# Linear attention and a state-space convolution on one core: rewritten with placed buffers and fixed engine orders, sign pairs, squared far rows, and the output weights folded into the key-value state

## The chip, the cores and the metric

The kernel runs on one core of one Trainium2 chip. The metric is the device time of one execution in microseconds (us). Every run also lists the span of the core (first to last instruction, about 2 us shorter than the time) and the mean clock that the throttle granted to TensorE, as a share of full speed. The engines are named as the profile names them: PE is TensorE, PEld its weight loads, DVE is VectorE, ACT is ScalarE, POOL is GpSimd and SP is SyncE, which here only issues transfers (DMAs).

## The reference

Two independent halves are computed and laid side by side in one bf16 output of 2048 x 896.

```python
# A: Hedgehog linear attention; S = 2048, D = 448, H = 16 heads of Dh = 28
q, k, v = heads(x @ wqkv)
pq = einsum("bhsd,hdf->bhsf", q, w_phi)              # pk the same from k
phi_q = concatenate([softmax(pq), softmax(-pq)])     # 56 features a head; phi_k the same
kv = einsum("bhsf,bhsd->bhfd", phi_k, v)
z  = einsum("bhsf->bhf", phi_k)
o  = (phi_q @ kv) / (phi_q @ z + 1e-6)
a  = o @ wo                                          # 448 x 448

# B: S4 convolution; D = 448 channels, N = 256 complex states, L = 2048
P = exp((dt * A)[:, :, None] * l)                    # l = arange(L), rounded to bf16
K = einsum("dn,dnl,dn->dl", C, P, dt * B).real
y = irfft(rfft(u, 2L) * rfft(K, 2L))[:L] + u * Dskip

out = concatenate([a, y], axis=-1)
```

Because the positions `l` are rounded to bf16, only 641 of them differ. The kernels build those rows of K as products of 16 "high" powers and 49 "low" powers for each state, summed over the states by 1792 small matmuls, and do the convolution with matrix DFTs.

## The kernel before

The attention's queries are done in four parts of 512 rows. The exponentials `EQ` stay unscaled. The numerators of the two softmax signs go through PE separately, VectorE scales each by its reciprocal denominator while it reads it from PSUM, the two results are transposed and added by matmuls, and only then multiplied by `wo`:

```python
def query_side(sc, more):
    EQ = sb("EQ", [112, 2, 4, 512], BF16, ...)
    ...                                          # projections, exponentials, denominators
    TT(out=SC, in0=rz, in1=den[:, 1]...)         # SC[row, t4, sign, head]: the scales
    for t4 in range(4):
        for s in range(2):
            pn = mmt([128, D_MODEL])
            for c in range(4):
                mm(pn[:, 112 * c:112 * c + 112], lhsT=EQ[:, s, c, ts], rhs=KVN[:, s, c, :, :], ...)   # L533
            TT(out=o..., in0=pn..., in1=SC[:, t4, s].unsqueeze(2).to_broadcast([128, 16, D_HEAD]), op=ALU.mult)   # L536
        ...                                      # po: transpose and add the two signs
        for c in range(4):
            mm(pf[:, :], lhsT=oT_[:, c, :], rhs=wo[:, c, :], ...)
        ...                                      # copy to bf16, store
```

The low powers are exponentials times rotations. For each sign and each of two planes there is one multiply over 15 rows and one over a single row:

```python
for j0, n, sgn in ((0, n1, -1), (n1, 1, -1), (0, n1, 1), (n1, 1, 1)):
    r = w_rows(j0, n, sgn)
    for cs_ in (1, 0):
        TT(out=W[:, c, cs_, r, :], in0=W[:, c, cs_ if sgn < 0 else 0, r, :], in1=T[:, cs_, j0:j0 + n, xs], op=ALU.mult)   # L423
```

When a group of columns of K is ready it is scattered by 24 transfers, 20 of them of 128 rows, from the small tile `Ts` to the layout `Kt` that the kernel spectrum reads:

```python
def scatter_k(gi, Ts, engs):                     # engs: [nc.sync], for the last group [nc.sync, nc.gpsimd]
    for kt, h0, h1, l0, l1 in K_ROWS:
        for g in range(4):
            engs[i % len(engs)].dma_start(out=dst(0, 128, kt, g), in_=Ts[32 * g + h0:32 * g + h1, l0:l1, :])   # L571
    ...                                          # 4 more of one row
```

Engine orders come from a scheduler that works with priorities. Of the transfers, 170 are issued by SyncE, 23 by GpSimd and 6 by ScalarE.

The softmax here doesn't subtract the row's maximum and nothing guards it: scores larger than these inputs give would overflow.

## Time and profile before

| | before |
|---|---|
| time, median of 3 | 370.31 us (369.35 to 370.82) |
| span of the profiled run, granted clock | 365.3 us, 0.865 |
| VectorE busy | 305.1 us, 84% |
| TensorE busy | 276.7 us, 76% |
| ScalarE busy | 216.2 us, 59% |

The first lines are from the page of the kernel before: busy time of each engine with its share of the span and its instructions; the busy share of VectorE in 40 slices of the span, in tenths (9 is 90% or more); and the chain of waits that ended last, by engine.

```profile
span 365.3 us, 8990 instructions
...
PE 276.7 (76%) x3780; PEld 198.5 (54%) x3780; DVE 305.1 (84%) x532; ACT 216.2 (59%) x389; POOL 18.8 (5%) x35
...
DVE  0899989999955889895698789989969979999971
...
PE 39%; DVE 27%; ACT 14%; DMA 13%; issue 4%; SPq 2%; DVEq 0%; ACTq 0%
```

VectorE is nearly full from one end to the other. The next lines are groups of VectorE's instructions by form, before: line, engine, operation, out<-in, shapes, count, then busy us, mean ns of one, and after the second bar the idle time just ahead of them and what ended it.

```profile
L536 DVE TENSOR_TENSOR sbuf<-mmt,sbuf 128x448 bf16<-128x448 f32 x32 | 19.4, 621 | 11.7 <-PE mmt L533 11.6
...
L423 DVE TENSOR_TENSOR sbuf<-sbuf 128x1680 bf16<-128x1680 bf16 x32 | 32.0, 1027 | 1.1 <-ACT sbuf L411 1.1
...
L614 DVE TENSOR_TENSOR sbuf<-sbuf 128x3584 bf16<-128x3584 bf16 x6 | 12.0, 2021 | 2.4 <-ACT sbuf L600 2.4
```

A multiply of 1680 elements takes 1027 ns and one of 3584 takes 2021 ns, so 0.52 ns an element plus 0.15 us each time: the same work in fewer instructions is cheaper. The scaling from PSUM (L536) costs 19.4 us and makes VectorE wait 11.6 us for matmuls. The waits of VectorE before (engine, line, what was waited for: us in total, times, longest) begin with that:

```profile
DVE sbuf L536 <- PE mmt L533: 11.6, 17, 2.8
DVE sbuf L498 <- DMA sbuf<-const: 6.4, 1, 6.4
```

Last, the view of line 571 before, for the window of 220 to 233.6 us: how long SyncE was busy with one issue of a group's 20 scatters (ns: minimum / median / maximum; first and last start in us).

```profile
L571 SPq DMA_DIRECT2D sbuf<-sbuf x20: 592/607/729, 220.3 to 232.9; - x20
```

One issue takes 0.6 to 0.7 us.

### The profile page before, as it was taken

How to read it: one execution, taken by the hardware profiler on the slowest of the kernel's cores; microseconds unless marked ns; L12 is line 12 of the kernel's file. 1: busy time of each engine (PE TensorE's matmuls, PEld its weight loads, DVE VectorE, ACT ScalarE, POOL GpSimd, SP SyncE). 2: the span in 40 equal slices, each digit the busy share in tenths (PEclk: the TensorE clock that was granted, in tenths of full speed). 3: DMA queues.
4: the chain of work that ended last, by engine and by line, in shares of the span. 5: the costliest groups of instructions: out<-in, count | busy, mean ns of one | idle time of the engine just before them, and what ended most of it. 6: DMA issues, size and time to landing. Idle time of an engine off the chain costs nothing.

```text
span 365.3 us, 8990 instructions
## 1 busy us (share of the span) xinstructions
PE 276.7 (76%) x3780; PEld 198.5 (54%) x3780; DVE 305.1 (84%) x532; ACT 216.2 (59%) x389; POOL 18.8 (5%) x35
## 2 busy tenths in 40 slices
PE   0675399999946769997776996769754696948994
PEld 0542275555533446565535774547643485937993
DVE  0899989999955889895698789989969979999971
ACT  1599878866676428975948559726587323213321
POOL 5000100000000000000000000002000000342000
PEclk9995569999985789999886998768985889996999
DMA  7971102200151101210001001125711309387005
GB/s 180 298 222 47 45 1 102 100 2 0 55 165 60 51 33 48 77 52 27 25 28 27 28 16 30 16 88 154 256 55 12 103 11 380 126 126 202 2 10 196
DMA packets 31584, 31.57 MB, mean 86 GB/s; under 512 B 10008, under 2 KB 30072, under 8 KB 31160
## 3 DMA queue, kind: packets, MB, share of 16 engines
q1 hardware_dynamic: 27000, 24.49, 22.7%
q0 software_dynamic: 1760, 5.36, 5.2%
q10 hardware_dynamic: 2784, 1.15, 1.3%
q8 instruction: 29, 0.48, 0.5%
q14 instruction: 11, 0.09, 0.1%
HBM read 23.07 MB, written 7.34 MB: 83 GB/s over the span
## 4 chain that ended last, share of the span: by engine, by line
PE 39%; DVE 27%; ACT 14%; DMA 13%; issue 4%; SPq 2%; DVEq 0%; ACTq 0%
PE kb L457 12%; DMA sbuf<-const 5%; PE mmt L597 5%; PE mmt L238 4%; DVE sbuf L479 4%; PE mmt L549 4%; PE yo L638 3%; PE mmt L505 3%; DMA sbuf<-in_B_u_dram 3%; DVE sbuf L423 3%; DVE sbuf L485 3%; DMA sbuf<-sbuf 3%; ACT sbuf L411 3%; DMA sbuf<-in_A_x_dram 2%; PE mmt L543 2%
## 5 line engine op out<-in xcount | busy, mean ns | idle before, releaser
L457 PE MATMUL kb<-sbuf 128*16 128x49 bf16 x1792 | 51.3, 274 | 4.1 <-issue 3.3
L597 PE MATMUL mmt<-sbuf 128*128 128x112 bf16 (+1 forms) x336 | 33.0, 261 | 21.4 <-ACT sbuf L600 10.0
L457 PEld LDWEIGHTS <-sbuf 128*16 128x16 bf16 x1792 | 41.4, 118 | 11.5 <-issue 9.2
L238 PE MATMUL mmt<-sbuf 128*128 128x448 bf16 x128 | 34.0, 390 | 10.6 <-DVE sbuf L226 7.5
L597 PEld LDWEIGHTS <-sbuf 128*128 128x128 bf16 x336 | 26.8, 111 | 27.9 <-issue 11.4
L423 DVE TENSOR_TENSOR sbuf<-sbuf 128x112 bf16<-128x112 bf16 (+1 forms) x64 | 36.9, 618 | 5.8 <-ACT sbuf L408 4.7
L429 DVE TENSOR_TENSOR sbuf<-sbuf 128x896 bf16<-128x896 bf16 (+1 forms) x48 | 35.6, 773 | 0.2
L600 ACT CAST sbuf<-mmt 128x448 bf16<-128x448 f32 x32 | 16.3, 548 | 25.2 <-PE mmt L597 25.2
L638 PE MATMUL yo<-sbuf 128*128 128x112 bf16 (+1 forms) x384 | 28.8, 228 | 2.6 <-DMA sbuf<-const 1.5
L536 DVE TENSOR_TENSOR sbuf<-mmt,sbuf 128x448 bf16<-128x448 f32 x32 | 19.4, 621 | 11.7 <-PE mmt L533 11.6
L638 PEld LDWEIGHTS <-sbuf 128*128 128x128 bf16 x384 | 26.2, 98 | 3.2 <-DMA sbuf<-const 1.7
L241 ACT CAST sbuf<-mmt 128x448 bf16<-128x448 f32 x32 | 17.3, 548 | 15.7 <-issue 7.2
L614 DVE TENSOR_TENSOR sbuf<-sbuf 128x1792 bf16<-128x1792 bf16 (+1 forms) x18 | 24.4, 1398 | 2.4 <-ACT sbuf L600 2.4
L411 ACT ACTIVATE sbuf<-arg 128x896 bf16<-128x896 f32 (+1 forms) x32 | 24.8, 863 | 1.5 <-PE kb L457 1.1
L645 ACT CAST sbuf<-yo 128x224 bf16<-128x224 f32 (+1 forms) x24 | 9.0, 410 | 24.9 <-PE yo L640 24.9
L508 ACT ACTIVATE sbuf<-mmt 112x512 bf16<-112x512 f32 x32 | 17.2, 600 | 10.5 <-PE mmt L505 10.3
L475 ACT ACTIVATE sbuf<-pkv 128x448 bf16<-128x448 f32 x32 | 16.1, 547 | 11.0 <-PE pkv L471 11.0
L238 PEld LDWEIGHTS <-sbuf 128*128 128x128 bf16 x128 | 12.6, 104 | 17.8 <-issue 9.4
L549 PE MATMUL mmt<-sbuf 112*128 112x448 bf16 x64 | 18.2, 409 | 4.9 <-ACT sbuf L545 4.9
L288 DVE TENSOR_TENSOR sbuf<-sbuf 128x1792 bf16<-128x1792 bf16 (+3 forms) x33 | 20.1, 610 | 0.8
L377 PE MATMUL arg<-sbuf 128*128 128x224 bf16 x128 | 20.4, 300 | 0.6 <-ACT sbuf L408 0.5
L505 PE MATMUL mmt<-sbuf 112*112 112x512 bf16 x64 | 19.3, 437 | 0.8 <-ACT sbuf L508 0.5
(113 smaller groups left out, 563.7 us busy)
## 6 DMA issues: line engine op xcount, KB each, us to landing
sbuf<-const SPq DMA_DIRECT2D x32, 224.0 KB
SUd<-sbuf SPq DMA_DIRECT2D x16, 224.0 KB
sbuf<-const SPq DMA_DIRECT2D x2, 1024.0 KB
sbuf<-in_A_x_dram SPq DMA_DIRECT2D x4, 448.0 KB
out_dram<-sbuf SPq DMA_DIRECT2D x16, 112.0 KB
sbuf<-SUd POOLq DMA_DIRECT2D x1, 1792.0 KB, 12.9
sbuf<-in_B_u_dram SPq DMA_DIRECT2D x4, 448.0 KB
sbuf<-SUd POOLq DMA_DIRECT2D x2, 896.0 KB, 9.7
```

What stands on the lines that cost most here:

```text
L238: mm(p[:, 0:D_MODEL].rearrange("p (q g x) -> p q g x", q=4, g=4), lhsT=G1[:, cp, jt, 128 * mt:128 * mt + 128], rhs=by_quarter(ab[:, cp ^ s ...
L288: TT(out=tmp, in0=src, in1=pw(1), op=ALU.mult)
L377: mm(p[:, e // 2, (e % 2) * QC:(e % 2 + 1) * QC], lhsT=PID[:, 4 * grp + e, :], rhs=src[:, part, cols], start=(part == 0), stop=(part == 1))
L411: act(dst.rearrange("p c (a b) x -> p a b c x", b=2), src.rearrange("p a b (c x) -> p a b c x", c=2), ACT.Exp, scale=float(sgn * f))
L423: TT(out=W[:, c, cs_, r, :], in0=W[:, c, cs_ if sgn < 0 else 0, r, :], in1=T[:, cs_, j0:j0 + n, xs], op=ALU.mult)
L429: TT(out=(t2[:, :, 0:n, :], dst)[1 - i], in0=src, in1=PW[512][:, i, cols].unsqueeze(1).unsqueeze(1).to_broadcast([128, 2, n, COLS]), op=AL ...
L457: mm(p[32 * g:32 * g + N_HI, qq * N_LO:(qq + 1) * N_LO], lhsT=U[qt % 2][c][:, :, ri, xc], rhs=W[:, c, ri, :, xc], start=(i == 0), stop=(i ...
L505: mm(p[:, :], lhsT=WpQ[:, dj, 112 * c:112 * c + 112], rhs=xT[:, dj, 512 * sc:512 * sc + 512], start=(dj == 0), stop=(dj == 3))
L549: mm(pf[:, :], lhsT=oT_[:, c, :], rhs=wo[:, c, :], start=(c == 0), stop=(c == 3))
L597: mm(p[:, k2, :].rearrange("p (q g x) -> p q g x", q=nq, g=4), lhsT=f_tiles[i][1][:, fi, :], rhs=natural(Kt[:, kt, :], gi), start=(n == 0) ...
L614: TT(out=t[:, :, :], in0=su, in1=sk, op=ALU.mult)
L638: mm(p[:, k2, :], lhsT=GI[r][:, cp, mt, 128 * jt:128 * jt + 128], rhs=S[:, r, cp, mt, :], start=(cp == 0 and mt == 0), stop=False)
```

## The change

The intent is to take work from VectorE, the fullest engine, and to fix by hand what a scheduler did: every buffer has a fixed address, every PSUM tile a fixed bank, and the instructions of all engines stand in one listed order. The main pieces are:

- The output weights are multiplied into the key-value state once (`M = kv @ wo` by head group). The scale of each query row and head must then be applied to `EQ` itself, ahead of one sum over both signs and all heads. `EQ` has head features on its partitions, so the scales, computed with rows on partitions, are transposed to `SCT` (32 pairs of sign and head x 512 rows) and spread to 28 partitions each by transfers: 8 per part, 32 in all. Then one multiply of 4096 elements scales a part.
- The low powers of both signs are multiplied together (3584 elements), more far rows come from squares, and the high tables are made for both halves of a quarter at once.
- The correction of one half of the signal by the other moves into matmuls; setup uses diagonal matmuls.
- Nearly all transfers are issued by SyncE: 234 of them; one is ScalarE's.

The diff is almost a rewrite; this is its core.

```diff
-            TT(out=o..., in0=pn..., in1=SC[:, t4, s].unsqueeze(2).to_broadcast([128, 16, D_HEAD]), op=ALU.mult)
-            ...                                  # 2 x 4 matmuls, a transpose pair and a copy for every 128 rows
+    p = PS("sct", [32, 4, 128], BF16)            # transpose SC; rows of SCT: (sign, head)
+    ...
+    vcopy(SCT, p)
+    for s in range(2):
+        for c in range(4):
+            h0 = 16 * s + 4 * c
+            dma(R[:, s, c, :], bc(SCT[h0:h0 + 4].rearrange("p t x -> p (t x)"), 1, D_HEAD))
+    mul(EQ..., EQ..., R...)                      # 112 x 4096
+    for t4 in range(4):
+        for i in range(8):
+            s, c = i // 4, i % 4
+            mm(pf, EQ[:, s, c, ts], M[:, s, c, :], start=(i == 0), stop=(i == 7))
...
+    E = W[:, 0, 0:32].rearrange("p (i s) x -> p i s x", s=2)
+    mul(W[:, 1, 0:32]..., E, T[:, 1:3]...)       # both signs: 3584 elements
+    mul(E, E, bc(T[:, 0], 2, 2))
...
-                engs[i % len(engs)].dma_start(out=dst(0, 128, kt, g), in_=Ts[...])
+                dma(dst(128, kt, g), Ts[...])
...
+    def dma(out, in_, eng=nc.sync):
+        P.op(lambda: eng.dma_start(out=out, in_=in_))
...
+    with tc.manual_schedule():
+        P.run(ORDER)                             # a list of 1383 numbers; ADDR and BANK place the buffers
```

`bc(ap, axis, n)` repeats an operand n times along a new axis with step 0.

## The prediction

> **What bounds it now.** The page gives VectorE 305 us busy of a 365.3 us span (84%), TensorE 277, ScalarE 216. In the forty-slice rows VectorE is at 8 or 9 tenths nearly everywhere; by the timeline its real work starts at 10 us (loads) and ends 7.6 us before the end. About 42 us of idle time lies between; the waits view names 11.6 us of the output scaling (L536) waiting for matmuls, 6.4 for a constant, 4.7 for signal loads, 4.7 for exponentials. TensorE is close behind: from 60 to 90 us it has 29.2 of 30, VectorE 28.4. The chain of waits mixes PE 39%, DVE 27%, ACT 14%, DMA 13%.
>
> **VectorE.** From the groups by form, a bf16 tensor-tensor costs 0.52 ns an element plus 157 ns (3584: 2021 ns, 448: 386); neighbours overlap by about 50 ns. [...] Instructions fall from 532 to 335. Estimates, us:
> - damping and far rows (sign pairs, squares): 95 to 82, with added negations at an estimated 0.6 each;
> - high tables, both halves at once: 66 to 54;
> - query: 32 PSUM scalings (19.4) become 4 multiplies of 4096 (9) and 4 copies: 28 to 20;
> - correction of y1 by y0 (4.6) moves to 16 matmuls;
> - setup by diagonal matmuls: 27 to 20;
> - key side 35 to 33; PSUM clearing 1 to 0.
>
> With less overlap: 262 busy, 43 less.
>
> **Others.** ScalarE loses sign copies (16), transposed-output copies (9.5), setup (4); gains 64 smaller table evaluations (15), squares and far copies (10), folded weights (5): about 217. TensorE loses 256 small query matmuls (L533, L543: 28), gains 64 output matmuls of 448 columns (0.21 each), doubles the weight loads of the arguments (13.8 now), adds the corrections: about 270. It becomes the longest sum[...].
>
> **Critical path.** The savings lie where VectorE is full, so they count unless TensorE replaces it. The fixed order interleaves the stages and holds output projections back to fill TensorE in the convolution. The waits of L536 vanish. Against it: a longer tail after VectorE's last product (about 40 projections and 108 inverse matmuls), nearly all DMAs in one in-order queue, orders that can't adapt. Sum: head 11 + VectorE 262 + tail 15 + inner stalls 25 (42 now) = 313.
>
> **Predicted 313 us, 80% range 296 to 338.** Faster by over 2%: 0.94; within 2%: 0.04; slower: 0.02.
>
> **What would show each step.** VectorE busy 255 to 270 in about 335 instructions; two 3584-element multiplies of 2.02 us for each of eight damping blocks; no PSUM scaling; inner VectorE idle below 30; ScalarE 210 to 225; TensorE 260 to 280, over 85% of the span; last VectorE work 12 to 18 before the end. Wrong steps would show as [...]negations well above 0.6 us.
>
> **What would make it wrong.** Fixed orders whose assumed durations differ from the chip's: waits at the head of in-order queues that give back 20 us or more (335). The DMA queue bringing the replicated scales or far rows late. A mean granted clock below 0.85 with TensorE the limit. On the other side, tight interleaving could leave VectorE nearly no inner idle time: 292 to 296.

The sum: 11 + 262 + 15 + 25 = 313. For some of its figures, this is what the traces show. On VectorE, 382 of the 531 neighbouring pairs before overlap, by 83 ns in the mean (31.7 us in all, which is 60 ns over all pairs; the prediction has about 50). Matmuls of 448 columns that follow each other and overlap start 0.21 us apart in the mean before (229 pairs, median 0.19). SyncE's 170 issues before and 234 after stand one behind the other, no two overlap. The 0.6 us of a negation is the author's estimate; the kernel after took 612 ns for one of 1792 elements.

## More of the kernel before

The view by stretches of 60 us, before, is for comparison later. Columns: stretch, us, then busy us (and instructions) of PE, PEld, DVE, ACT and POOL, granted clock, DMA share, GB/s.

```profile
180.00:240.00 60.00, 47.64 (x733) 32.41 (x733) 55.10 (x109) 40.31 (x69) 0.00 (x0) 0.85 0.13 32
240.00:300.00 60.00, 41.79 (x835) 33.59 (x834) 51.84 (x92) 32.24 (x55) 2.27 (x2) 0.78 0.31 92
```

VectorE has 46 to 56 us of work in every such stretch up to 360 us.

## The result, and the profile after

The kernel after takes 389.9 us (median of 4 runs, 387.09 to 392.85) against 369.83 us (4 runs) of the kernel before. The ratio is 1.0548, with a 95% interval of 1.0481 to 1.0615: slower. Executions over 1.5% slower than the fastest of the same kernel are left out of the means. Ratios here and below compare the two kernels in the same rounds, so they are not quite the ratio of the medians.

The same lines of the page, after:

```profile
span 385.3 us, 8823 instructions
...
PE 253.5 (66%) x3744; PEld 186.7 (48%) x3744; DVE 259.1 (67%) x335; ACT 211.1 (55%) x440; POOL 4.2 (1%) x30
...
DVE  3773999999999998999588800069990006505980
...
SPq 29%; DVE 25%; PE 23%; DMA 12%; ACT 6%; issue 4%; DVEq 0%; ACTq 0%
```

VectorE's work fell from 305.1 to 259.1 us, and the span still grew by 20 us. The row of slices has something that the row before has not: slices of 0 in its second half. And SyncE's issuing, 2% of the chain before, is its largest member at 29%. The stretches after, with the same columns:

```profile
60.00:120.00 60.00, 56.84 (x710) 34.60 (x712) 59.93 (x72) 51.37 (x111) 0.45 (x3) 1.00 0.31 78
120.00:180.00 60.00, 42.42 (x1025) 34.95 (x1016) 57.87 (x76) 53.26 (x110) 1.56 (x8) 0.77 0.07 14
180.00:240.00 60.00, 36.62 (x690) 29.64 (x686) 31.35 (x40) 31.39 (x67) 0.51 (x3) 0.81 0.33 79
240.00:300.00 60.00, 28.59 (x474) 23.26 (x474) 33.72 (x30) 11.54 (x22) 0.00 (x0) 0.73 0.48 145
```

Up to 180 us the change does what it was meant to do: VectorE is full (59.93 of 60 us). From there on, when the queries and the scatters of K begin, no engine is busy for more than 36.6 of 60 us. The groups of VectorE by form, after:

```profile
L268 DVE TENSOR_TENSOR sbuf<-sbuf 128x3584 bf16<-128x3584 bf16 x38 | 75.9, 2015 | 4.9 <-DMA sbuf<-SUd 3.5 <-ACT sbuf L296 1.0
...
L268 DVE TENSOR_TENSOR sbuf<-sbuf 112x4096 bf16<-112x4096 bf16 x4 | 9.1, 2287 | 49.1 <-DMA sbuf<-sbuf 49.1
```

The large multiplies cost what was predicted. But the four scalings of the queries, 9.1 us of work, had 49.1 us of idle time ahead of them, ended by transfers between on-chip buffers. The first line of VectorE's waits after gives the whole sum:

```profile
DVE sbuf L268 <- DMA sbuf<-sbuf: 79.3, 4, 30.4
```

These are three stalls in VectorE's timeline after (start us, us, instruction; in brackets the idle time just ahead):

```profile
250.48 0.29 DVE L268 TENSOR_TENSOR sbuf<-psum,sbuf 128x128 f32<-128x128 f32 x1 [29.79 <-DMA sbuf<-sbuf]
...
318.48 2.83 DVE L268 TENSOR_TENSOR sbuf<-sbuf 112x4096 bf16<-112x4096 bf16 x2 [30.44 <-DMA sbuf<-sbuf]
...
350.94 22.89 DVE L268 TENSOR_TENSOR sbuf<-sbuf 112x4096 bf16<-112x4096 bf16 x28 [18.63 <-DMA sbuf<-sbuf]
```

The last two wait for their own scales. The first waits for scales of another part. In the list of addresses, its output `dz` lies in the memory of a `SCT` that 8 copies, issued from 202.7 to 244 us, were still reading. A placed buffer hides such a dependence: nothing in the code of that multiply names the copies. By itself the shared address cost little here: the next multiply, at 250.69 us, is the scaling that needs the same 8 copies, so VectorE would have stalled there.

What SyncE did then is in the chain of waits after, in order of time (start us, us, what), ahead of the second stall:

```profile
302.94 2.27 SPq L308
305.21 0.04 issue
305.25 2.24 SPq L308
...
310.96 7.40 DMA sbuf<-sbuf
...
318.48 2.30 DVE sbuf L268
```

One issue takes over 2 us where a scatter of the kernel before needed 0.6 to 0.7. The view of the line that issues all transfers, after, shows that it was not always so (durations of one in ns: minimum / median / maximum; first and last start):

```profile
L308 SPq DMA_DIRECT2D sbuf<-sbuf x104: 545/658/3650, 164.1 to 349.9; - x104
```

Half of the 104 on-chip copies (72 scatters and 32 of scales) are issued in 0.66 us or less, and the longest takes 3.65 us. The same view for 325.5 to 344.3 us holds 8 copies of scales and no scatter:

```profile
L308 SPq DMA_DIRECT2D sbuf<-sbuf x8: 1594/1978/3454, 325.7 to 342.5; - x8
```

None of these takes less than 1.59 us. The 72 scatters take 0.94 us each in the mean (67.9 us in all, from the issue records), where those above took 0.6 to 0.7: most of them take as long as before (median 0.62 us), but 8 take over 1.3 us. Summed over the issue records of the trace, SyncE spends 92.5 us on 170 issues before and 209.4 us on 234 issues after. Issues longer than 1.3 us number 3 before (7.1 us) and 40 after (99.2 us): 18 of the 32 scale copies, 8 scatters and 14 other transfers.

The packet records of the trace give the other half. The packets of the scale copies, 1024 B each, last 90 ns in the mean. At least one is in flight for 99.1 us in all, and while that is so there are 3.2 in flight in the mean and never more than 6: 3.67 MB in 99.1 us is 37 GB/s. Eight of the copies run with no other scale copy in flight; these take 3.8 to 4.6 us for their 114,688 B, which is 25 to 30 GB/s. The source of a copy has 4 rows outermost; whether that is why so few are in flight, the experiments have to show. The trace does not number the DMA engines.

### The profile page after: what moved, and what is told of

It is laid out like the page before. It is cut to its first block, busy times and chain, and to the rows that moved or that the text cites. A ratio compares the mean times of both kernels' runs of the same rounds, so it can differ in the third digit from the quotient of the medians.

```text
span 385.3 us, 8823 instructions
## 1 busy us (share of the span) xinstructions
PE 253.5 (66%) x3744; PEld 186.7 (48%) x3744; DVE 259.1 (67%) x335; ACT 211.1 (55%) x440; POOL 4.2 (1%) x30
## 4 chain that ended last, share of the span: by engine, by line
SPq 29%; DVE 25%; PE 23%; DMA 12%; ACT 6%; issue 4%; DVEq 0%; ACTq 0%
SPq L308 29%; PE psum L302 23%; DVE sbuf L268 23%; DMA sbuf<-sbuf 6%; DMA sbuf<-in_B_u_dram 3%; ACT sbuf L296 3%; ACT sbuf L299 3%; DMA sbuf<-in_A_x_dram 2%; DMA sbuf<-in_B_log_dt_dram 1%; DVE sbuf L280 1%; DVE sbuf L288 1%; DVE sbuf L592 1%; ACT L296 0%; DVE sbuf L283 0%; DVE sbuf L292 0%
## 5 line engine op out<-in xcount | busy, mean ns | idle before, releaser
L302 PE MATMUL psum<-sbuf 128*16 128x49 bf16 (+9 forms) x3624 | 245.2, 273 | 126.6 <-DMA sbuf<-sbuf 52.2
L302 PEld LDWEIGHTS <-sbuf 128*16 128x16 bf16 (+4 forms) x3624 | 178.6, 114 | 191.8 <-issue 76.0
L268 DVE TENSOR_TENSOR sbuf<-sbuf 128x448 bf16<-128x448 bf16 (+9 forms) x247 | 213.7, 919 | 70.5 <-DMA sbuf<-sbuf 49.6
L299 ACT CAST sbuf<-psum 128x448 bf16<-128x448 f32 (+3 forms) x156 | 83.4, 591 | 120.1 <-PE psum L302 109.4
L296 ACT ACTIVATE sbuf<-psum 128x448 bf16<-128x448 f32 (+5 forms) x200 | 92.9, 566 | 7.7 <-PE psum L302 5.4
L296 ACT ACTIVATE sbuf<-sbuf 128x896 bf16<-128x896 bf16 (+2 forms) x11 | 11.5, 1045 | 42.4 <-DVE sbuf L268 40.7
L296 ACT ACTIVATE sbuf<-psum,sbuf 128x112 bf16<-128x112 f32 (+4 forms) x48 | 26.7, 617 | 0.0
L592 DVE TENSOR_REDUCE sbuf<-sbuf 128x64 f32<-128x1792 bf16 x8 | 16.0, 2007 | 0.0
L305 PE MATMUL psum<-sbuf 128*112 128x128 bf16 (+2 forms) x120 | 11.1, 243 | 1.8 <-DMA sbuf<-in_A_x_dram 1.3
L305 PEld LDWEIGHTS <-sbuf 128*112 128x112 bf16 (+2 forms) x120 | 9.4, 148 | 3.0 <-DMA sbuf<-in_A_x_dram 1.8
```

Source lines behind the costliest of these rows:

```text
L268: P.op(lambda: nc.vector.tensor_tensor(out=out, in0=in0, in1=in1, op=op))
L296: P.op(lambda: nc.scalar.activation(out, in_, func, scale=float(scale), **kw))
L299: P.op(lambda: nc.scalar.copy(out, in_))
L302: P.op(lambda: nc.tensor.matmul(out, lhsT=lhsT, rhs=rhs, start=start, stop=stop, **kw))
L305: P.op(lambda: nc.tensor.transpose(out, in_, identity))
L592: P.op(lambda zk=zk, EK=EK: nc.vector.tensor_reduce(zk.rearrange("p i s h -> p (i s) h"), EK.rearrange("p i s (h f) -> p (i s) h f", f=D_H ...
```

## The experiments

Three theories were set against each other.

- **A, slow copies.** The 32 copies of scales are slow by their shape (4 rows outermost, with 3.2 packets in flight in the mean; all reads from those 4 on-chip rows), and as SyncE issues nearly all transfers one after another (234 issues after, no two overlapping), everything behind them is late.
- **B, many issues.** It is the count: 234 issues in one queue, whatever they carry.
- **C, the fixed orders.** The order or the lower granted clock (0.826 against 0.865) costs the time, and the waits for copies only show where.

Each experiment is an edit of the kernel after. Every verdict is against the kernel before on the same chip; its median was 369.6 to 370.0 us throughout. The kernel after itself was timed in the first round only, so differences to its 389.9 us lean on the kernel before having stayed the same. Where an expectation has a cut, its ground was an assumption on how many DMA engines such a copy uses, which no trace here shows; what rested on it alone (5 to 20 us for kt_pool) was the author's guess. The results in one table:

| kernel | edit | median us | ratio to before (95%) | result |
|---|---|---|---|---|
| after | none | 389.9 | 1.0548 (1.0481 to 1.0615) | correct |
| no_r | scale copies replaced by constants | 318.39 | 0.8612 (0.8573 to 0.8651) | wrong |
| kt_pool | scatters of K issued by GpSimd | 355.41 (3 runs; 355.77 of all 4) | 0.9590 (0.9517 to 0.9664) | correct |
| r_pool | scale copies issued by GpSimd | 358.71 | 0.9712 (0.9666 to 0.9759) | correct |
| row_pool | the same, four per copy | 362.94 | 0.9834 (0.9784 to 0.9884) | correct; unclear against before, as the interval holds 0.98 |
| hop4 | scales by way of DRAM, 4 outermost | 341.03 | 0.9208 (0.9146 to 0.9270) | correct |
| hop14 | scales by way of DRAM, 28 outermost | 328.85 | 0.8909 (0.8841 to 0.8977) | correct |
| hop_kt | by way of DRAM, 4 copies a part, scatters by GpSimd | 317.78 | 0.8621 (0.8581 to 0.8661) | correct |
| no_r_kt | no_r and kt_pool | 314.10 | 0.8498 (0.8460 to 0.8536) | wrong |
| hop_kt2 | hop_kt, scatters by SyncE and GpSimd in turn | 317.26 | 0.8573 (0.8541 to 0.8606) | correct |

### no_r: without the copies

```diff
-                dma(R[:, s, c, :], bc(SCT[h0:h0 + 4].rearrange("p t x -> p (t x)"), 1, D_HEAD))
+                gset(R[:, s, c, :], 1.0)        # GpSimd writes ones: wrong result on purpose
```

> The 32 copies that spread the query scales over the heads' rows are replaced by fills of 1.0 from GpSimd; the result is wrong on purpose. Theory A (these copies[...] hold up everything behind them in the one DMA queue): VectorE's waits for on-chip copies, 79 us in the changed kernel, fall below 20 and the time falls to 295 to 320 us. Rival B (what costs is the number of issues on one queue, about 0.6 us each, whichever they are): 32 of 234 issues go, so 32 x 0.6 = about 20 us less, 365 to 375. Rival C (fixed orders built on wrong durations and a lower granted clock): within 2% of the changed kernel, 382 to 398.

Measured: 318.39 us. The order of all other instructions is as it was, 202 issues remain on SyncE, and the granted clock is 0.903. From its VectorE waits:

```profile
DVE sbuf L268 <- DMA sbuf<-sbuf: 2.9, 2, 1.8
```

VectorE has the same 259.1 us of work, and the waits for on-chip copies go from 79.3 to 2.9 us. The 72 scatters of K, still in SyncE's queue, no longer delay it. The sum of SyncE's issues falls from 209.4 to 121.1 us, and those over 1.3 us from 40 to 8. Of this, 49.5 us and 18 long issues were the copies' own; the 202 issues that remain fell from 159.8 to 121.1 us, and from 22 long ones to 8. B and C fall as the main cause: by count alone 32 of 234 issues can't be worth 71 us, and the orders are the same. The clock rose when only the copies went, so its fall in the kernel after is not a cause that stands by itself; how much of the 71 us came by way of the clock is not shown (TensorE's busy time fell by 6.5 us, from 253.5 to 247.0).

### kt_pool and r_pool: the two kinds of copies in two queues

```diff
 # kt_pool
-                dma(dst(128, kt, g), Ts[32 * g + h0:32 * g + h1, l0:l1, :])
+                dma(dst(128, kt, g), Ts[32 * g + h0:32 * g + h1, l0:l1, :], nc.gpsimd)
 # (and the four single rows)
 # r_pool
-                dma(R[:, s, c, :], bc(SCT[h0:h0 + 4]..., 1, D_HEAD))
+                dma(R[:, s, c, :], bc(SCT[h0:h0 + 4]..., 1, D_HEAD), nc.gpsimd)
```

> The 72 scatters of kernel rows are issued from GpSimd's queue; the scale copies stay as they are. Rival B: 72 x 0.6 = 43 us of issue time leave the queue, and the time falls to 340 to 350. Theory A: [...]a gain of 5 to 20 us at most, 368 to 388.

> The 32 scale copies keep their shape (four source rows each, on chip) and are issued from GpSimd's queue instead of the shared one. If the copies harm mainly because they hold the shared queue in order: the shared queue's issues longer than 1.3 us (40 in the changed kernel) fall below 10, and the time comes near the run without the copies, 318 to 335 us. If it is the transfers themselves[...]: 1024-byte packets still take about 90 ns with 3 to 4 in flight, VectorE still waits over 30 us for them, 340 to 370 us.

Measured: 355.41 us and 358.71 us. Either way of parting the two kinds of copies is worth 31 to 34 us, and either leaves 37 to 40 us to no_r. Parting the queues therefore mattered more than theory A had said for kt_pool and less than B had; it is about half of the loss. From r_pool's VectorE waits:

```profile
DVE sbuf L268 <- ACT sbuf L299: 33.6, 3, 30.0
...
DVE sbuf L268 <- DMA sbuf<-sbuf: 21.3, 3, 10.7
```

The long wait has moved to a ScalarE result, which has its own wait further back; PE waits 58.5 us for on-chip copies in that run. The time fell in the second range expected of r_pool, but most of the details did not come: VectorE waits 21.3 us for on-chip copies and not over 30, and the packets are others. GpSimd's queue makes packets of 4096 B of the same copies; each lasts 628 ns, 10.3 are in flight in the mean, and the copies are in flight for 54.5 us at 67 GB/s. So r_pool changed the packets along with the queue, and its gain can't be put down to the queue alone. The first guess failed too. SyncE no longer issues any scale copy, and still has 18 issues over 1.3 us (22 in the kernel after, the scale copies left out). Its view of the scatters in r_pool:

```profile
L308 SPq DMA_DIRECT2D sbuf<-sbuf x72: 544/629/6422, 163.5 to 304.3; - x72
```

The longest takes 6.42 us, and 12 of the 72 take over 1.3 us: slow copies from another queue make SyncE's issues long as well (18 of 202 here, against 8 of 202 in no_r). Nor is the issuing small beside the transfers: the 72 scatters take 67.9 us to issue in the kernel after, while packets of their sizes are in flight for at most 27.2 us, and moving these issues to GpSimd is worth 34 us.

### row_pool: a source of one row each

```diff
-                dma(R[:, s, c, :], bc(SCT[h0:h0 + 4].rearrange("p t x -> p (t x)"), 1, D_HEAD))
+                with P:
+                    for h in range(4):
+                        r = 16 * s + 4 * c + h
+                        dma(R[28 * h:28 * h + 28, s, c, :], bc(SCT[r:r + 1].rearrange("p t x -> p (t x)"), 1, D_HEAD), nc.gpsimd)
```

The aim was more packets in flight at once with the on-chip source kept: with one row, the 28 repeats come outermost.

> Each scale copy is cut into four, one source row and 28 target rows each (128 copies, GpSimd's queue)[...], but all of them read one row of on-chip memory. If the number of engines is what limits: 10 or more packets in flight, total time of these packets below 50 us, 325 to 340 us. If the reads of one row are what limits: packets of over 150 ns, total time of these packets still 80 us or more, 340 to 380 us. 128 issues on GpSimd at about 0.6 us are 77 us of an engine that is idle otherwise.

Measured: 362.94 us, no better than r_pool. The packet records show 8.5 packets in flight, but a packet of 2048 B lasts 454 ns, and the copies are in flight for 95.2 us: 38.5 GB/s, as slow as in the kernel after with its 3.2 packets in flight. The copies' own wait in row_pool's VectorE waits stays large:

```profile
DVE sbuf L268 <- DMA sbuf<-sbuf: 37.3, 4, 17.4
```

So more packets at once did not help here, where each copy reads one row of on-chip memory (8.5 in flight and 38.5 GB/s, against 3.2 and 37 GB/s in the kernel after). The copies that ran alone in the kernel after moved 25 to 30 GB/s. The 37, 38.5 and 67 GB/s over all copies (after, row_pool, r_pool) lie above it; in the kernel after, the other 24 of the 32 copies overlap. What limits the reading of few on-chip rows is not shown. The cost of GpSimd's 128 issues (65.3 us, 0.51 each; the median of its 23 in the kernel before was 0.60) is mixed into this experiment.

### hop4 and hop14: a source in DRAM, and the shape

```diff
+        hop = dram.tile([32, 512], BF16, ...)
+        copy(hop, SCT)                                               # 1 transfer, 32 KB
-                dma(R[:, s, c, :], bc(SCT[h0:h0 + 4]..., 1, D_HEAD))  # 8 of these
 # hop4: 8 copies as before, 4 rows outermost in the source
+            copy(R[:, i // 4, i % 4, :], bc(hop[4 * i:4 * i + 4], 1, D_HEAD))
 # hop14: 8 copies, 28 outermost on both sides
+            copy(R[28 * h:28 * h + 28, s, :, :], bc(hop[16 * s + h:16 * s + 16:4], 0, D_HEAD))
```

All stay on SyncE, in the same places of the order; each part has one more issue than after.

> The scales go to DRAM once for each quarter, and eight copies spread them from there, each with a source whose outermost size is still 4. Theory A: still about 4 packets in flight in these copies, 370 to 400 us. If the slow part was only that on-chip source (all reads from four rows of the same memory): faster packets and 320 to 350. Rival B: 36 issues in place of 32, so slightly slower than the changed kernel, 388 to 396.

> As hop4, with the same number of copies, packets and bytes, but each copy's outermost size is 28 on both sides. Theory A: [...]issues in the region back to about 0.6 us, and 300 to 325 us. Rival B and rival C: no difference to hop4, 385 to 396.

Measured: hop4 341.03 us and hop14 328.85 us. With the same division into 4, the DRAM source alone is worth 49 us; the mean packet goes from 90 to 49 ns and the time in flight from 99.1 to 46.7 us (3.67 MB in that time is 79 GB/s; the time includes the packets that write `hop`). Three of its copies run with no other in flight; they take 1.5 to 2.4 us, against 3.8 to 4.6 us from the chip. The number of packets in flight is still 3.9. The outermost 28 brings 8.3 packets in flight, 29.2 us and 126 GB/s, and another 12 us of time. Theory A held for the cause but had its two parts in the wrong proportion: in this order of changing them, the few source rows on the chip (49 us) weigh more than the small outermost size (12 us). Its number for hop14 (300 to 325 us) was missed. VectorE waits 29.1 us for the scales in hop4; from hop14's VectorE waits:

```profile
DVE sbuf L268 <- DMA sbuf<-hop: 23.1, 3, 13.7
```

The scales are still late, but less so. And the scatters of K, which were not touched, are issued faster, as the view of the issuing line shows for hop14:

```profile
L308 SPq DMA_DIRECT2D sbuf<-sbuf x72: 545/613/1219, 163.2 to 266.9; - x72
```

The longest is 1.22 us, against 3.65 in the kernel after. Both kernels issue 238 transfers, more than the kernel after: the issues over 1.3 us go 40, 11, 5 and the sum of issue time 209.4, 157.0, 136.6 us (after, hop4, hop14). So it is not the count that made the issues long here, but the slow transfers.

### hop_kt: both, with fewer copies

```diff
+        for h in range(4):                       # 4 copies a part, each 28 outermost
+            copy(R[28 * h:28 * h + 28].rearrange("p s c x -> p (s c) x"), bc(hop[h:32:4], 0, D_HEAD))
+                dma(dst(128, kt, g), Ts[...], nc.gpsimd)             # as in kt_pool
```

> A version meant to be used: the DRAM hop[...], now four of 28 x 8 rows for each quarter, and the 72 scatters of kernel rows on GpSimd's queue. Against the hop with eight copies (329 us): 16 + 72 issues fewer on the shared queue, 88 x 0.6 = 53 us of issue time; if the rest of the loss is that queue, 300 to 318 us. If the scatters no longer matter once the scale copies are quick: 322 to 332.

Measured: 317.78 us (6 runs, 316.56 to 320.55), correct, and 14% below the kernel before. It is as fast as no_r, which moves no scales at all. Against hop14, three things changed (4 copies in place of 8, all issued in the first three of the eight places of the order, and the scatters' queue); no run parts them. From hop_kt's page (busy, chain):

```profile
PE 244.9 (77%) x3744; PEld 182.8 (58%) x3744; DVE 259.4 (82%) x335; ACT 210.8 (67%) x440; POOL 45.3 (14%) x102
...
PE 28%; DVE 27%; DMA 22%; issue 9%; ACT 5%; SPq 5%; POOL 3%; DVEq 0%; POOLq 0%; ACTq 0%
```

SyncE's issuing has 5% of the chain, and the engines' work is unchanged. The waits of VectorE in hop_kt that were the largest:

```profile
DVE sbuf L268 <- PE psum L302: 8.1, 2, 7.6
DVE sbuf L268 <- DMA sbuf<-hop: 7.9, 3, 5.8
```

And the stretch that was half empty, in hop_kt:

```profile
180.00:240.00 60.00, 49.30 (x983) 38.48 (x980) 46.61 (x58) 36.94 (x77) 14.22 (x26) 0.91 0.63 186
```

VectorE does 46.61 us of work there instead of 31.35.

### no_r_kt and hop_kt2: what is left

no_r_kt puts the scatters on GpSimd in no_r; hop_kt2 lets SyncE and GpSimd take the scatters in turn in hop_kt:

```diff
 # no_r_kt = no_r, and
+                dma(dst(128, kt, g), Ts[...], nc.gpsimd)
 # hop_kt2 = hop_kt, but
+                dma(dst(128, kt, g), Ts[...], (nc.sync, nc.gpsimd)[g % 2])
```

> Both at once: no scale copies (wrong on purpose) and the scatters on GpSimd's queue. It shows what is left when neither is in the shared queue. If the good version (318 us) still loses time to the scale copies: 295 to 308 us. If the copies through DRAM are by now free and something else holds the rest: 312 to 320 us.

> As the good version, but the scatters alternate between the shared queue and GpSimd's, since its chain of waits has 28% in landings of on-chip copies and GpSimd issues one in 0.5 us. If the issue time of the 20 large scatters of a group is what holds the kernel-spectrum matmuls: 4 to 8 us faster, 308 to 315. If it is what was scattered late, or the landing time: within 1% of 318.

Measured: 314.10 and 317.26 us. Without scale copies, the scatters' queue is worth 318.39 - 314.10 = 4.3 us, against 34 us with them. The two costs are not independent: the scatters are delayed by the copies ahead of them. The second result is within 1% of hop_kt: dealing the scatters out among two queues, and not to GpSimd alone, makes no difference. (The 28% in its expectation are of the chain from 180 us on; GpSimd's issues in hop_kt took 0.60 us in the median, 0.52 at the least.) With hop_kt 3.7 us above no_r_kt, there is little left to gain from the copies (no_r_kt has GpSimd write the ones, so it isn't quite the floor).

## Why the prediction was wrong

Predicted were 313 us (296 to 338), with 0.02 for slower; measured were 389.9 us.

- **VectorE's work: right.** Predicted 262 us in about 335 instructions; measured 259.1 in 335. Multiplies of 3584 take 2015 ns (2.02 us predicted), negations 612 ns (0.6), and no scaling from PSUM is left. A multiply has a fixed part of 0.15 us (1027 ns for 1680 elements and 2021 for 3584 in the trace before); the saving by fewer, larger instructions came as reckoned in the sum.
- **ScalarE: right** (217, measured 211.1). **TensorE: too high** (270, range 260 to 280; measured 253.5). At 66% of the span it was not the limit, where the prediction had over 85%.
- **"The savings lie where VectorE is full, so they count": this step failed.** Up to 180 us it held: VectorE did 160.7 us of work by then against 142.4 before (sums of the stretches). The kernel then had only 259.1 - 160.7 = 98.4 us of work left and took 205 us for it, because VectorE stopped being the limit.
- **"inner stalls 25 (42 now)": the term that was mis-sized.** Span less busy time, less about 4.4 us ahead of VectorE's first work (11 predicted) and 11.5 after its last, is 385.3 - 259.1 - 15.9 = 110 us. Of that, 79.3 us are waits for on-chip copies.
- **"32 PSUM scalings (19.4) become 4 multiplies of 4096 (9) and 4 copies": a cost left out.** VectorE's side of it was right (9.1 us). But to bring the scales to where that multiply reads them takes 32 transfers, and the prediction gave them no time. This is the step that failed first; the other two follow from it in the main. Its risk paragraph named "the DMA queue bringing the replicated scales or far rows late", and sized queue waits at 20 us or more (335). Taking the copies out was worth 389.9 - 318.4 = 71.5 us. Their sizes could have been read in the diff: a source of 4 rows read 28 times, 3.67 MB in all, in the queue that also carries 72 scatters. What was not to be had from the trace before is their speed, 37 GB/s.
- **Tail: nearly right** (12 to 18 us after VectorE's last work, measured 11.5).

hop_kt, which differs from the kernel after only in how scales and scatters travel, takes 317.8 us, within the range predicted. Its span is 316.0 us: 259.4 us of VectorE's work, about 15.7 at both ends, and 41 us of idle time within. So even with quick copies the sum comes near 313 partly by luck: the idle time within is 16 us over the 25 of the prediction, and the ends (26 predicted) and VectorE's work (262) make up 13 us of it.

**How far the cause is shown.** Shown are: the copies cost 71.5 us (no_r); moving one kind of copy to GpSimd's queue regains 31 to 34 (kt_pool, r_pool; in r_pool the packets changed with it); the source's place 49 (hop4), the outermost size another 12 (hop14, in that order of changing them). The parts overlap and can't be added: the scatters' queue is worth 34 us with the slow copies and 4.3 us without them. That slow transfers make other issues of SyncE long is shown by the untouched scatters: 3.65 us at the most behind slow copies in their own queue, 6.42 us beside slow copies in GpSimd's (r_pool), 1.22 us with quick ones in their own (hop14). By what means the issuer is held is not shown.

**Still open.** How much of row_pool and r_pool is GpSimd's issuing, how much the other packets and how much the source. Which DMA engines carried the packets, and how many: only packets in flight are recorded. What sets the granted clock, 0.826 in the kernel after and about 0.9 in the fast variants. And what the 41 us of idle time within hop_kt would take; fewer orders fixed by assumption would be the next thing to try.

## What to carry to other kernels

Cost a new transfer as you would an instruction: its outermost size on both sides (4 to 28 was worth 12 us here), how many source rows it reads and from where (49 us), its bytes, the queue it is put in, and what else has to be issued while it runs (31 to 34 us for parting the two kinds of copies). When the engines' busy times come out as predicted and the time doesn't, look at who issues: the share of the issuing queue in the chain, and issues that take longer than the same kind took elsewhere. A broadcast of few on-chip rows to many partitions was faster here by way of DRAM, with a large number outermost, than straight from the chip (328.9 us in hop14 against 389.9).
